# A delta-rule attention and a multiplicative FFN on one core: a new list of the early steps, and the last product's two token blocks summed and stored one by one

## The chip, the cores and the metric

The kernel runs on one core of one Trainium2 chip. The metric is device time in microseconds of one execution, and the time of a kernel is the median of its runs. One of the executions of the kernel before was recorded by the profiler; all durations below come from that one.

## What is computed

Two blocks follow each other. The first is a delta-rule recurrence over 768 time steps, for 4 batches of 8 heads with 48 features; the second multiplies the result, as 3072 tokens of 384 features, with four weights.

```
k_n = k / (norm(k) + 1e-6)
for t in range(768):
    y[t] = q[t] @ state
    v_old = k_n[t] @ state
    state += beta[t] * outer(k_n[t], v[t] - v_old)
x = y as (3072 tokens, 384)
a, b = x @ w1, x @ w2                  # 384 x 1024 each
out = ((a * b) @ w3) @ w_out           # 1024 x 1024, 1024 x 384
```

All data are float32.

## The kernel before

**Tiling.** The sequence is cut into 12 chunks of 64 time steps. Two chunks make a unit, so there are six units, of 512 tokens each. Within a chunk the recurrence is solved in matrix form: scores K K^T and Q K^T, the inverse of a triangular matrix, and a chain that carries the state from chunk to chunk. In the FFN, `w3 @ w_out` is folded once into one weight `w34` of 1024 x 384, so that a unit needs the two products with w1 and w2 (eight column slabs of 128), their elementwise product, and one product with `w34`. That last product is done in a scheme with seven half-size products in place of eight (`slab_sums`, `weight_sums`, `o`), whose results are combined by additions in `result`.

**One list sets the order on every engine.** The kernel is a set of Python generators, one for each piece of work, and the string `ORDER` (line 39) names which of them does its next step. `in_text_order` (line 159) then ties every engine's instructions to the order of the text. So an engine that waits for one step holds up all later steps of its own queue. SyncE (SP), which issues nearly all DMAs, is such a queue too. The names in the list:

- `P0` to `P7`: a 128-row piece of w_out; `P8` to `P23`: half of a 128-row block of w3; `P24` to `P29`: pieces of w1, `P30` to `P35`: pieces of w2 (`piece`, line 695). Each piece has four steps: its DMA into a buffer `raw`; two activations on ScalarE (ACT, lines 707 and 708); two operations on VectorE (DVE, lines 710 and 711); an addition on GpSimd (POOL, line 715). There are five `raw` buffers in turn, so that the load of a piece waits until the POOL step of the piece five places before it is done.
- `t`: transposes of w3 on TensorE (PE), `f0` to `f7`: the folds into `w34` (line 756), each in two halves; the first half needs P0 to P3, the second P4 to P7.
- `k`, `q`, `v`, `p`: loads of a chunk; `K`, `Q`, `d`: the transposed keys and queries, by PE for the first two chunks, by DVE later; `g` and `N`: squared norms and their inverse roots.
- `s`: scores; they leave `U` (DVE, line 379) and the masked `PT` (ACT copy and POOL multiplication for the first two chunks). `u`: `U` to DRAM in blocks; `V0` to `V5`: the triangular inverse of a unit, 31 pairs of DVE operations (lines 440 and 445), after a load of `Ub` and followed by a store of `Vd`; `e`: the rest of the inverse, which begins with eight DMAs from `Vd`.
- `n`: values times norms (POOL); `c`: the chain; `y`: a chunk's outputs on PE, eight ACT copies into `xT`, and six small DMAs within `xT` (line 684).
- `b0` to `b7`: a slab of unit 0 for chunk 0 alone (N = 256 columns); `a00` to `a07`: the same for chunk 1; `a10` and so on: a slab of a later unit, both chunks (line 772).
- `T`: the weight sums, `S`: the slab sums (both POOL), `o`: the seven products of a unit (line 851), `x`: their sums and stores (`result`, line 896).

**The end.** For the last unit `o` puts the products named E and F into two-bank PSUM buffers of their own. `store` (line 880) takes the next of two SBUF buffers `osb`, lets `make` fill its 384 columns (two token blocks of 192), and issues two DMAs, one for each token block. Of the last unit's four stores, three are sums on DVE, one after the other: U3 + C, U3 - D, and M1 + F, where F is the product that PE does last.

Of the kernel before, what the change touches and what calls it, by code (L numbers as in the profile page):

```python
# [45 lines left out]
P16 V0 f0 f1 P14 t11 V0 V0 f0 f1 v1 P15 P15 v0 P15 t6 t11 V0 V0 V0 V0 P16 f5 V0 P20 g1 P22 s1
P21 t8 P23 P22 t6 d2 f5 f5 P20 d2 P20 V0 P21 P15 n0 t7 P24 V0 f3 V0 t9 t8 V0 t7 t9 s2 P20 V0 n0
V0 f4 p3 n1 P22 P23 V0 V0 V0 P23 g1 d3 V0 V0 P22 g1 f3 t14 P23 f4 f3 t12 t14 P30 f4 p3 g1 V0
t15 n1 t12 P26 s1 g1 g1 f6 f7 e0 d3 N1 e0 t15 e0 P21 e1 N1 f7 e0 P21 p4 s2 d3 P24 s2 P24 e0 s2
e1 s2 e0 s2 d3 e1 P30 e1 c0 c0 f7 s3 V1 u2 P26 y0 t13 P24 P26 s3 P31 s3 P26 N1 P30 P30 y0 s3  # L50
P25 c0 P31 P25 s3 u3 s3 c0 t13 e1 c1 P31 e1 c1 P32 V1 c1 P25 V1 P28 c1 P31 V1 V1 V1 V1 V1 V1 V1
f6 V1 V1 P32 V1 V1 P32 y0 f6 V1 V1 V1 P25 P28 P28 V1 V1 v2 y1 b2 b2 b0 P32 y1 b3 b3 P27 P29 b3
b0 b0 V1 b0 b1 y1 c1 k4 a00 b1 P28 b3 P29 n2 P29 P27 P27 V1 a01 P33 a00 a00 a03 P27 V1 V1 V1 V1
a00 a02 V1 P29 V1 V1 V1 V1 a01 a03 V1 V1 b5 g2 P33 P34 a02 b5 b7 k5 a07 b2 V1 V1 P35 a06 b7 V1
b2 p4 b6 P34 g2 a06 a07 V1 n2 a04 V1 b4 b6 P33 P35 a05 g2 P34 b4 b1 c1 g2 V1 P34 a04 e2 P35 a01
P33 P35 a05 g2 a01 e3 T d4 e2 a03 c2 e2 b1 c2 e2 g2 d4 d4 g2 a04 T p5 e2 e2 d4 a05 g2 a03 a04
c2 s4 c2 g2 b5 g2 p5 a05 N2 b4 s4 s4 c2 a06 b5 c2 b4 a07 y2 d5 y2 s4 d5 T b7 s4 a02 s4 a06 b6
S0 d5 e3 v3 d5 a02 T a07 b6 S0 e3 e3 n3 V2 n3 s5 k6 g3 b7 s5 s5 S0 S0 g3 o0 c3 u4 c3 s5 N2 e3
e3 s5 S0 g3 s5 u5 x0 S0 S0 V2 o0 S0 c3 S0 c3 S0 S0 o0 x0 y3 x0 V2 V2 S0 V2 V2 V2 g3 y3 N2 o0 S0
v4 o0 c3 V2 V2 x0 V2 V2 V2 S0 V2 y3 o0 V2 S0 x0 x0 p6 V2 x0 x0 a10 V2 x0 S0 o0 V2 x0 V2 V2 a10  # L60
a16 a16 a15 a12 p6 V2 V2 a10 a11 a12 V2 k7 V2 V2 v5 g3 V2 V2 V2 a15 V2 a11 V2 a14 a17 V2 a10 x0
V2 V2 V2 d6 a12 a17 d6 g3 V2 g3 g3 e4 a14 d6 e4 a17 e4 a13 c3 c4 n5 a17 e4 a12 n4 V3 n4 g3 p7
d6 e4 g3 c4 e4 n5 a14 s6 N3 a13 s6 c4 a11 s6 a14 c4 c4 p7 y4 c4 e5 d7 a15 e5 y4 k8 e5 c5 c5 g4
d7 g4 a13 a16 e5 d7 d7 a15 a13 v6 a16 a11 s7 e5 S1 g4 g4 s7 o1 p8 s7 S1 e5 x1 s7 s7 S1 s7 c5 o1
s6 S1 u7 c5 o1 s6 s6 u6 S1 S1 V3 S1 y5 c5 c5 V3 V3 V3 V3 V3 o1 S1 x1 k9 S1 y5 S1 y5 o1 S1 S1 x1
x1 V3 S1 S1 V3 c6 V3 S1 S1 V3 d8 o1 x1 x1 v7 a20 n6 x1 V3 a20 o1 x1 a23 V3 V3 x1 V3 x1 n7 a27
a24 d8 a26 V3 V3 V3 V3 x1 g4 V3 a23 V3 a25 V3 a27 a27 V3 a24 V3 V3 a26 a20 V3 g4 V3 p8 V3 V3 V3
V3 p9 V3 V3 a25 d8 n6 d8 g4 a20 a22 a22 a24 V3 c6 a27 a25 a24 a21 a21 e6 e6 e6 g4 e7 N3 e6 a25
N3 g4 s8 g4 N4 s8 e6 a22 s8 a26 e6 c6 c6 N4 s8 a26 s8 y6 a22 V4 p9 N4 S2 d9 e7 s8 a21 e7 y6 u8
d9 a21 e7 c6 a23 d9 p10 e7 d9 S2 c6 S2 s9 n7 a23 s9 e7 o2 s9 c7 s9 S2 s9 k10 S2 c7 x2 o2 c7 S2  # L70
S2 o2 u9 s9 V4 c7 V4 S2 y7 V4 V4 x2 V4 g5 g5 V4 p10 d10 y7 S2 x2 S2 o2 y7 V4 o2 x2 c7 V4 V4 S2
S2 V4 o2 a35 x2 x2 k11 x2 S2 V4 x2 S2 a35 v8 V4 S2 V4 V4 S2 V4 x2 n8 o2 a37 x2 V4 v9 V4 V4 V4
x2 a34 n8 V4 V4 a36 a30 V4 V4 V4 V4 V4 a37 V4 a34 a33 V4 g5 a33 a30 a32 a36 V4 V4 V4 V4 a34 a33
V4 V5 a32 e8 n9 c7 e8 a30 c8 a33 e8 e9 e8 g5 a35 a34 c8 a30 e8 g5 d10 a32 e9 g5 a32 g5 a36 e8
e9 S3 c8 a36 a35 a31 d10 d10 e9 a31 n9 c8 g5 c8 c8 g5 g5 e9 a31 s10 N5 e9 p11 s10 s10 a31 c9
a37 a37 p11 c9 y8 N5 v11 d11 S3 d11 d11 o3 v10 d11 s10 y8 s10 S3 u10 S3 s11 N5 s11 o3 s10 c9
s11 c9 s11 S3 x3 S3 s11 o3 S3 S3 y9 o3 s11 x3 S3 o3 u11 V5 S3 S3 V5 y9 V5 x3 n11 S3 x3 V5 V5 V5
S3 y9 S3 S3 V5 c9 V5 o3 x3 V5 x3 x3 V5 V5 x3 S3 a47 o3 x3 V5 V5 a47 x3 V5 V5 a47 n10 V5 a46 a40
a40 V5 a47 V5 a43 V5 a46 x3 a42 a45 V5 a42 V5 a41 a45 a43 V5 V5 V5 V5 V5 V5 a44 V5 a44 V5 a45
a41 V5 V5 V5 V5 c9 a42 e10 a40 e10 n11 a42 e10 a44 e10 c10 a45 n10 e11 e10 e11 c10 a43 e10 c10  # L80
c10 a40 e11 a41 a46 e11 c10 a44 S4 a43 e11 a41 S4 c10 o4 e11 a46 c11 x4 S4 S4 y10 o4 c11 c11 S4
y10 S4 S4 S4 S4 S4 c11 o4 y11 o4 x4 S4 S4 S4 o4 y11 x4 x4 o4 S4 x4 x4 S4 y11 S4 x4 x4 a50 x4 o4
a50 x4 a55 a56 a55 a52 a55 a50 a52 a56 a54 a57 a54 a55 a54 a50 a54 a51 a52 a57 a51 a53 x4 a52
a53 a51 a56 a56 a53 a51 a53 a57 o5 S5 a57 S5 S5 o5 S5 S5 S5 x5 S5 S5 S5 o5 o5 x5 S5 S5 S5 o5 S5
S5 S5 o5 x5 S5 x5 o5 x5 x5 x5 x5 x5 x5 x5 x5
"""


# [1 line left out]
def kernel(  # L90
# [799 lines left out]

    last = NCH // 2 - 1

    def bank_of(u, n):
        return banks[u, n].rearrange("p b d -> p (b d)")

    def result(u):
        def plus(x, n, op=ALU.add):
            return lambda o_: dve.tensor_tensor(  # L898
                out=o_, in0=ws_[x], in1=bank_of(u, n), op=op
            )  # L900
# [134 lines left out]
```

## Time and profile before

| | us |
|---|---|
| median of 3 runs (591.1 to 597.29) | 592.53 |
| the profiled execution | 597.89 |
| its span, from first to last instruction | 596.2 |
| PE busy in the span | 545.3 |
| DVE busy in the span | 363.5 |
| ACT busy in the span | 158.8 |
| POOL busy in the span | 176.3 |
| matmuls with w1 and w2 (line 779), busy | 129.6 and 131.4 |
| matmuls of the seven products (line 873), busy | 65.0 and 49.6 |

The profiled execution lies 1.69 us over its span, and 5.36 us over the median of the three runs. The matmuls of line 779 are single instructions of 538 ns, pipelined, so that their busy times overlap a little. The page also gives the busy share of every engine in 40 slices of about 15 us; there DVE, POOL and the DMA engines are at their busiest in the first ten slices and PE from the tenth slice on.

### The profile page before, as it was taken

The numbers are of one execution on the slowest core, as the hardware profiler recorded it, in microseconds if no ns is written. First come the engines' busy times: TensorE is split into PE (matmuls) and PEld (weight loads), VectorE is DVE, ScalarE is ACT, GpSimd is POOL, SyncE is SP. The second block draws the span as 40 slices with busy tenths as digits, with TensorE's granted clock in tenths as the row PEclk, the third lists the DMA queues.
The fourth block names the chain that finished last, engine by engine and source line by source line (L and its number), as shares of the span: only waits on it lengthen the run. The fifth ranks groups of instructions, "written<-read, shape, count | busy, mean of one in ns | idle before, by whom it ended". The sixth has DMA issues, their size and how long they took to land.

```text
span 596.2 us, 19061 instructions
## 1 busy us (share of the span) xinstructions
PE 545.3 (91%) x8188; PEld 381.0 (64%) x8188; DVE 363.5 (61%) x827; ACT 158.8 (27%) x333; POOL 176.3 (30%) x223
## 2 busy tenths in 40 slices
PE   2477999578999999999999989999999999999996
...
DVE  3887997568877579665697555875746924110012
...
PEclk9998999878999899999999999999999999999999
DMA  9989986776856255553463345614333040010001
GB/s 247 186 175 266 216 155 132 129 156 120 166 81 101 70 103 93 99 92 50 110 112 73 53 70 98 130 47 72 57 65 90 13 89 4 16 46 8 1 0 53
DMA packets 219507, 57.31 MB, mean 96 GB/s; under 512 B 206656, under 2 KB 212800, under 8 KB 219424
## 3 DMA queue, kind: packets, MB, share of 16 engines
...
q10 hardware_dynamic: 4192, 0.79, 0.9%
...
## 4 chain that ended last, share of the span: by engine, by line
PE 78%; DMA 10%; SPq 5%; DVE 3%; issue 2%; ACT 1%; POOL 1%; ACTq 0%; DVEq 0%; POOLq 0%
PE ps_f L779 41%; PE ps_f L873 19%; PE ps_w L551 5%; DMA raw<-in_moe_w_dram 4%; PE ps_w L652 4%; PE ps_f L759 3%; PE ps_w L498 3%; SPq L230 2%; PE ps_w L367 2%; PE ps_w L373 2%; DMA ktok<-in_k_dram 1%; DMA Ub<-Ud 1%; DMA Ud<-U 1%; SPq L699 1%; DMA X<-in_q_dram 1%
## 5 line engine op out<-in xcount | busy, mean ns | idle before, releaser
L779 PE MATMUL ps_f<-xT,w1s 128*128 128x512 f32 (+1 forms) x336 | 129.6, 538 | 2.6 <-DMA xT<-xT 2.6
L779 PE MATMUL ps_f<-xT,w2s 128*128 128x512 f32 (+1 forms) x336 | 131.4, 537 | 0.0
L846 POOL TENSOR_TENSOR ab<-ab 128x256 f32<-128x256 f32 x96 | 67.1, 727 | 193.6 <-DVE ab L795 167.8
L779 PEld LDWEIGHTS ps_f<-xT,w1s 128*128 128x128 f32 x336 | 64.3, 193 | 58.1 <-issue 53.7
L779 PEld LDWEIGHTS ps_f<-xT,w2s 128*128 128x128 f32 x336 | 62.2, 190 | 53.7 <-issue 50.2
L791 ACT COPY ab<-ps_f 128x512 f32<-128x512 f32 (+1 forms) x56 | 28.3, 526 | 172.3 <-PE ps_f L779 168.1
L873 PE MATMUL ps_f<-w,ab 128*128 128x192 f32 x368 | 65.0, 330 | 0.0
L795 DVE TENSOR_TENSOR ab<-ab,ps_f 128x512 f32<-128x512 f32 (+1 forms) x56 | 32.7, 603 | 48.8 <-PE ps_f L779 48.6
L873 PEld LDWEIGHTS ps_f<-w,ab 128*128 128x128 f32 x368 | 59.7, 190 | 3.9 <-issue 2.9
L440 DVE TENSOR_TENSOR tb<-Vb,Ub 128x31 f32<-128x31 f32 (+15 forms) x124 | 45.8, 370 | 14.3 <-DMA Ub<-Ud 10.9
L873 PE MATMUL ps_f<-room,ab 128*128 128x192 f32 x272 | 49.6, 337 | 0.8 <-DVE room L898 0.8
L759 PE MATMUL ps_f<-w2s,w3T 128*128 128x384 f32 x128 | 46.3, 515 | 3.4 <-POOL w2s L715 3.3
L445 DVE TENSOR_TENSOR Vb<-Vb,tb 128x31 f32<-128x31 f32 (+15 forms) x124 | 46.4, 374 | 4.3
L873 PEld LDWEIGHTS ps_f<-room,ab 128*128 128x128 f32 x272 | 45.8, 195 | 1.6 <-issue 1.1
L673 ACT COPY xT<-ps_w 48x256 f32<-48x256 f32 x96 | 30.4, 365 | 52.5 <-PE ps_w L652 52.0
L759 PEld LDWEIGHTS ps_f<-w2s,w3T 128*128 128x128 f32 x128 | 24.7, 200 | 20.3 <-POOL w2s L715 4.2
L270 POOL TENSOR_TENSOR sq<-ktok 128x384 f32<-128x384 f32 x24 | 20.6, 863 | 57.6 <-DMA ktok<-in_k_dram 27.5
L367 PE MATMUL ps_w<-KQ 48*64 48x128 f32 x384 | 30.4, 298 | 1.1 <-ACT KQ L347 1.1
L373 PE MATMUL ps_w<-KQ 48*64 48x64 f32 x768 | 30.7, 236 | 0.0
L715 POOL TENSOR_TENSOR w<-w,raw 128x512 uint32<-128x512 uint32 x16 | 20.8, 1307 | 32.2 <-DVE w L711 13.5
L537 POOL TENSOR_TENSOR vtok<-vtok,n 128x384 f32<-128x384 f32 x24 | 20.1, 849 | 33.7 <-DMA vtok<-in_v_dram 33.7
L373 PEld LDWEIGHTS ps_w<-KQ 48*64 48x64 f32 x768 | 27.8, 149 | 0.1
...
## 6 DMA issues: line engine op xcount, KB each, us to landing
...
```

Source lines behind the costliest of these rows:

```text
L367: pe.matmul(ps[half(z), 0, n : n + 128], lhsT=x[:, 0, :], rhs=x.rearrange("p j t -> p (j t)"), start=True, stop=True,)
L373: pe.matmul(ps[half(z ^ j), 1, n + C * j : n + C * j + C], lhsT=x[:, 0, :], rhs=x[:, j, :], start=True, stop=True,)
L440: dve.tensor_tensor(out=tv, in0=V[:, 0 : s + 1, s : s + 1].to_broadcast([P, s + 1, n]), in1=U[:, s, s + 1 : BS].unsqueeze(1).to_broadcast( ...
L445: dve.tensor_tensor(out=o, in0=o, in1=tv, op=ALU.subtract)
L551: pe.matmul(out(ps, r, h, z), lhsT=lhs(r, h, z), rhs=rhs(r, h, z), start=True, stop=True,)
L673: act.copy(out=xT[f, p:NP:2, b : b + NR, cc, :].rearrange("p a r t -> p r a t"), in_=pyv[f, z, b : b + NR],)
L759: pe.matmul(ps[:, 0:DM], lhsT=w3Ts[jc, kc // 4][:, kc % 4 * P : kc % 4 * P + P], rhs=wo[:, kc], start=(kc == 0), stop=(kc == KF - 1),)
L779: pe.matmul(ps[:].rearrange("p b c t -> p b (c t)"), lhsT=w[:, m, js], rhs=x[:, m, :, c0:c1].rearrange("p b c t -> p b (c t)"), start=(m = ...
L791: act.copy(out=t, in_=ps)
L795: dve.tensor_tensor(out=t, in0=t, in1=ps, op=ALU.mult)
L846: pool.tensor_tensor(out=o_, in0=x_, in1=y_, op=op)
L873: pe.matmul(ps[:, b, :], lhsT=abs_[u, HF * f + i][:, t0 : t0 + P], rhs=ws_[w][:, i], start=first and b == i == 0, stop=i == HF - 1 and b = ...
```

## The change

The list in `ORDER` is another one up to a place in the middle of unit 1's products and the first of its outputs; after it the names are the same ones in the same order, but for one more `x5` at the end. No name appears more or less often in the early part, so every instruction of it is still there; only the order on the engines is another.

On the engines this comes to the following. **SP:** nearly the same order of transfers. What differs: a piece of w_out changes places with pieces of w3 among the first loads, and two pieces of w_out stand after the permuted loads `p2`, not before them; one piece of w1 stands ahead of `u2`; `k4` and `k5` stand after the pieces P33 to P35; later the DMAs of `e4` and `e5` stand together, ahead of loads that were between them. **The pieces** of one kind are taken in another sequence: before P6 P10 P8 P2 P11 P13 P12 P18 P9 P7 P1 P3 P0 P5 P4, after P0 P18 P13 P11 P10 P3 P12 P8 P9 P2 P5 P1 P4 P6 P7. **PE:** the first halves of f1, f0 and f2 stand together ahead of the first second half (before: f1, f2, then the second half of f2); after y1 the six half-slab products are b3 b1 b0 b1 b2 b3 (before b2 b0 b3 b3 b0 b1). **ACT:** P15 stands after the copies of f1 and t11 (before after f2, f0 and f1); P30 stands ahead of e0's first copies; e1's last copies stand directly after P25 and P31 (before t13 lay between). **DVE:** seven pieces stand between the first and the last pair of V0 (before eight). **POOL:** V0's two memsets stand ahead of the first piece (before after the first two products of g0); the pieces P25 and P30 stand ahead of s1's second mask multiplication.

The core of the list, its first lines:

```diff
-k0 P6 beta P10 P6 beta P6 P8 P6 P2 P11 K0 P10 P13 k1 P10 K0 P2 beta P11 q0 P10 P12 g0 P2 P8 P11
-g0 g0 P13 K1 V0 g0 P2 P12 K0 P8 P11 K0 K0 K1 K1 P8 g0 P12 P13 g0 Q0 g0 g0 g0 Q0 Q0 P13 P18 g0
-Q0 P9 Q0 K1 P12 s0 k2 P18 N0 q1 s0 K1 P7 P1 g1 s0 s0 P9 g1 Q1 Q1 Q1 Q1 P18 Q1 s0 s0 s0 P7 P18
+V0 P0 k0 beta P18 P13 P0 P18 P0 P0 P18 P18 g0 P11 beta P13 K0 K0 P11 P10 q0 P10 P3 k1 P11 P13
+K0 beta P12 g0 P3 K0 g0 K0 g0 P13 K1 g0 P8 P12 g0 K1 K1 P11 P9 Q0 Q0 g0 Q0 P10 P12 g0 Q0 Q0 g0
+k2 K1 s0 g0 P9 P10 P8 N0 K1 q1 P2 s0 N0 P3 Q1 s0 P12 p2 g1 Q1 P2 N0 s0 s0 Q1 P9 Q1 P8 Q1 g1 s0
...
```

The second part of the change is in `o`, `store` and `result`. F's two token blocks go into two PSUM banks, each with its own start and stop; the sum M1 + F is made and stored in two parts of 192 columns, into the buffer of U2, which no one reads any more then, and not into an `osb`.

```diff
-            if first and n in "EF":
-                banks[u, n] = two_banks()[:, 0, 0 : HB * HD].rearrange(
-                    "p (b d) -> p b d", b=HB
-                )
-            elif first:
-                banks[u, n] = bank([P, HB, HD])[:]
+            if first:
+                ps = [bank([P, HB, HD])[:]] * HB if n not in "EF" else [
+                    two_banks()[:, 0, 0 : HB * HD].rearrange("p (b d) -> p b d", b=HB)
+                ] * HB
+                if n == "F":
+                    ps[0] = bank([P, HB, HD])[:]
+                banks[u, n] = ps
...
-                        start=first and b == i == 0,
-                        stop=i == HF - 1 and b == HB - 1, skip_group_check=not first,
+                        start=first and i == 0 and (b == 0 or n == "F"),
+                        stop=i == HF - 1 and (b == HB - 1 or n == "F"),
+                        skip_group_check=not first,
...
-    def store(u, z, d, make):
-        osb = in_turn(ffn, [P, DM], "o", 2, "osb")
-        make(osb[:])
-        yield
-        for b in range(HB):
-            t0 = (HB * z + b) * S + u * 2 * C
-            sync.dma_start(
-                out=out[t0 : t0 + P, d_half(d)], in_=osb[:, HD * b : HD * b + HD]
-            )
-        yield
+    def store(u, z, d, make, osb=None, parts=1):
+        if osb is None:
+            osb = in_turn(ffn, [P, DM], "o", 2, "osb")[:]
+        n = DM // parts
+        for i in range(0, DM, n):
+            make(osb[:, i : i + n], slice(i, i + n))
+            yield
+            for b in range(i // HD, (i + n) // HD):
+                t0 = (HB * z + b) * S + u * 2 * C
+                sync.dma_start(
+                    out=out[t0 : t0 + P, d_half(d)], in_=osb[:, HD * b : HD * b + HD]
+                )
+            yield
...
-        yield from store(u, 0, 1, plus("M1", "F") if u == last else plus("U2", "C"))
+        if u == last:
+            yield from store(u, 0, 1, plus("M1", "F"), ws_["U2"], HB)
+        else:
+            yield from store(u, 0, 1, plus("U2", "C"))
```

More of the change, by code (lines that the diff above doesn't have):

```diff
@@ L39 @@
 ORDER = """
-k0 P6 beta P10 P6 beta P6 P8 P6 P2 P11 K0 P10 P13 k1 P10 K0 P2 beta P11 q0 P10 P12 g0 P2 P8 P11
-g0 g0 P13 K1 V0 g0 P2 P12 K0 P8 P11 K0 K0 K1 K1 P8 g0 P12 P13 g0 Q0 g0 g0 g0 Q0 Q0 P13 P18 g0
-Q0 P9 Q0 K1 P12 s0 k2 P18 N0 q1 s0 K1 P7 P1 g1 s0 s0 P9 g1 Q1 Q1 Q1 Q1 P18 Q1 s0 s0 s0 P7 P18
-g1 P3 P9 t2 P7 s1 s1 s1 s1 s1 s1 P7 P1 t2 P3 t5 P1 p2 d2 N0 t5 N0 P0 P0 P3 P0 u0 P9 d2 u1 P1 P3
-P5 t1 P4 g1 P0 t0 V0 V0 t0 P19 t1 t10 t3 P5 t4 V0 P14 P16 f1 P5 V0 V0 V0 V0 V0 P4 P4 V0 t10 t4
-f2 V0 P19 V0 t3 P14 P5 P14 P19 P17 P17 k3 s0 p2 P4 P16 V0 P17 V0 V0 V0 V0 f2 f2 f0 P17 V0 P19
@@ L46 @@
[L46 to L85, printed above, removed]
+V0 P0 k0 beta P18 P13 P0 P18 P0 P0 P18 P18 g0 P11 beta P13 K0 K0 P11 P10 q0 P10 P3 k1 P11 P13
+K0 beta P12 g0 P3 K0 g0 K0 g0 P13 K1 g0 P8 P12 g0 K1 K1 P11 P9 Q0 Q0 g0 Q0 P10 P12 g0 Q0 Q0 g0
@@ new lines @@
+k2 K1 s0 g0 P9 P10 P8 N0 K1 q1 P2 s0 N0 P3 Q1 s0 P12 p2 g1 Q1 P2 N0 s0 s0 Q1 P9 Q1 P8 Q1 g1 s0
+P3 s0 t2 t2 t3 s1 P5 P8 P2 g1 s1 P2 P1 s1 s1 t3 P9 P5 s1 P4 s1 P5 u0 P5 s1 d2 P1 P4 t1 u1 t0 P6
+t4 P7 t1 t10 P1 t0 t5 V0 t4 P14 g1 V0 P1 t10 P6 f1 t5 V0 d2 P4 P6 V0 V0 V0 P7 V0 P7 V0 P16 P14
+V0 P4 V0 P19 P19 P19 P6 f0 P16 P17 P17 V0 V0 P16 V0 V0 P17 P7 f2 k3 P14 p2 V0 V0 v1 P19 P15 f1
+f0 g1 f1 t11 V0 d2 t11 P15 f2 f5 V0 P14 P15 f0 P16 v0 P17 V0 V0 V0 V0 g1 P20 f5 V0 f2 f5 t6 t9
+P15 t6 P20 t7 V0 n1 P22 P20 V0 t7 d2 s0 V0 V0 f3 P23 P20 P22 t8 P21 V0 n0 P24 n0 f3 V0 V0 n1 t8
@@ new lines @@
+V0 V0 t9 V0 V0 s2 p3 f4 f3 P23 P22 P26 g1 V0 g1 V0 f4 g1 P21 P22 P23 t14 d3 f4 P23 g1 t12 p3 V0
+N1 P30 t12 t14 t15 e0 t15 d3 f7 d3 f6 e0 P30 P21 e0 e0 P24 f7 s2 s2 e1 e0 s2 P24 e0 e1 V1 p4 s2
+e1 P26 s2 e1 P25 d3 c0 P21 P30 u2 s3 c0 s3 P26 N1 P31 P24 y0 s3 s3 y0 c0 s3 s3 P25 t13 N1 e1 u3
+P31 c0 P26 P31 P32 c1 V1 c1 e1 P25 V1 P27 c1 V1 c1 V1 V1 t13 V1 V1 V1 V1 V1 V1 y0 V1 P25 f7 f6
+f6 P30 P32 P32 v2 V1 P27 s1 P31 V1 V1 y1 b3 b1 V1 b0 P32 P28 y1 b1 V1 b1 b3 P29 P27 b2 b3 y1 V1
+P27 b1 b0 P29 P29 c1 a01 b2 a03 P28 V1 a01 a00 b3 P28 P29 a02 a02 a03 P35 P28 V1 a05 b7 a00 V1
@@ new lines @@
+V1 V1 V1 a06 P33 V1 b5 a05 b7 b0 V1 P34 V1 b5 V1 a06 V1 V1 V1 P34 k4 V1 P35 V1 g2 a00 V1 k5 a00
+b0 V1 V1 g2 a04 P34 n2 p4 n2 a07 c1 a04 b2 b4 P33 b6 b2 P35 V1 g2 g2 P34 g2 e2 a07 g2 P33 e2
+P35 c2 c2 e3 d4 a03 d4 a03 a01 P33 g2 b4 d4 g2 e2 b6 e2 a07 e2 b4 d4 T a01 T b4 e2 a07 c2 s4 p5
+g2 c2 T g2 N2 V2 b6 p5 b6 s4 b5 s4 c2 a06 c2 a06 a04 v3 y2 d5 b5 d5 k6 s4 e3 d5 s4 y2 a02 a05
+d5 s4 b7 a04 n3 S0 a02 a05 S0 s5 S0 u4 e3 s5 n3 s5 e3 b7 T o0 c3 c3 s5 g3 s5 S0 N2 N2 x0 e3 g3
+e3 o0 s5 c3 c3 u5 o0 x0 V2 S0 x0 y3 V2 y3 S0 V2 S0 V2 S0 S0 V2 V2 V2 S0 g3 o0 S0 o0 S0 x0 V2 c3
@@ new lines @@
+o0 v4 y3 V2 V2 V2 x0 p6 V2 x0 V2 S0 a10 a10 S0 g3 S0 x0 V2 x0 S0 o0 x0 x0 p6 a14 V2 k7 a17 a17
+a14 V2 V2 V2 a15 a16 V2 a16 a15 V2 g3 V2 V2 V2 V2 V2 v5 V2 x0 a13 V2 V2 V2 a17 a12 V2 a13 g3 V2
+V2 g3 a17 c3 a14 a13 d6 d6 a11 V2 e4 n4 a12 e4 e4 c4 d6 V3 e4 a14 a10 n4 g3 d6 c4 e5 a11 e4 s6
+g3 a13 e4 a12 p7 a10 c4 g3 N3 s6 c4 s6 a11 y4 n5 y4 c4 e5 a12 c4 a11 a15 c5 n5 e5 p7 a16 d7 d7
+d7 d7 o1 c5 v6 a16 k8 g4 g4 e5 g4 p8 a15 g4 s7 s7 S1 e5 s7 S1 e5 x1 s7 s7 S1 s7 c5 o1 s6 S1 u7
+c5 o1 s6 s6 u6 S1 S1 V3 S1 y5 c5 c5 V3 V3 V3 V3 V3 o1 S1 x1 k9 S1 y5 S1 y5 o1 S1 S1 x1 x1 V3 S1
@@ new lines @@
+S1 V3 c6 V3 S1 S1 V3 d8 o1 x1 x1 v7 a20 n6 x1 V3 a20 o1 x1 a23 V3 V3 x1 V3 x1 n7 a27 a24 d8 a26
+V3 V3 V3 V3 x1 g4 V3 a23 V3 a25 V3 a27 a27 V3 a24 V3 V3 a26 a20 V3 g4 V3 p8 V3 V3 V3 V3 p9 V3
+V3 a25 d8 n6 d8 g4 a20 a22 a22 a24 V3 c6 a27 a25 a24 a21 a21 e6 e6 e6 g4 e7 N3 e6 a25 N3 g4 s8
+g4 N4 s8 e6 a22 s8 a26 e6 c6 c6 N4 s8 a26 s8 y6 a22 V4 p9 N4 S2 d9 e7 s8 a21 e7 y6 u8 d9 a21 e7
+c6 a23 d9 p10 e7 d9 S2 c6 S2 s9 n7 a23 s9 e7 o2 s9 c7 s9 S2 s9 k10 S2 c7 x2 o2 c7 S2 S2 o2 u9
+s9 V4 c7 V4 S2 y7 V4 V4 x2 V4 g5 g5 V4 p10 d10 y7 S2 x2 S2 o2 y7 V4 o2 x2 c7 V4 V4 S2 S2 V4 o2
@@ new lines @@
+a35 x2 x2 k11 x2 S2 V4 x2 S2 a35 v8 V4 S2 V4 V4 S2 V4 x2 n8 o2 a37 x2 V4 v9 V4 V4 V4 x2 a34 n8
+V4 V4 a36 a30 V4 V4 V4 V4 V4 a37 V4 a34 a33 V4 g5 a33 a30 a32 a36 V4 V4 V4 V4 a34 a33 V4 V5 a32
+e8 n9 c7 e8 a30 c8 a33 e8 e9 e8 g5 a35 a34 c8 a30 e8 g5 d10 a32 e9 g5 a32 g5 a36 e8 e9 S3 c8
+a36 a35 a31 d10 d10 e9 a31 n9 c8 g5 c8 c8 g5 g5 e9 a31 s10 N5 e9 p11 s10 s10 a31 c9 a37 a37 p11
+c9 y8 N5 v11 d11 S3 d11 d11 o3 v10 d11 s10 y8 s10 S3 u10 S3 s11 N5 s11 o3 s10 c9 s11 c9 s11 S3
+x3 S3 s11 o3 S3 S3 y9 o3 s11 x3 S3 o3 u11 V5 S3 S3 V5 y9 V5 x3 n11 S3 x3 V5 V5 V5 S3 y9 S3 S3
@@ new lines @@
+V5 c9 V5 o3 x3 V5 x3 x3 V5 V5 x3 S3 a47 o3 x3 V5 V5 a47 x3 V5 V5 a47 n10 V5 a46 a40 a40 V5 a47
+V5 a43 V5 a46 x3 a42 a45 V5 a42 V5 a41 a45 a43 V5 V5 V5 V5 V5 V5 a44 V5 a44 V5 a45 a41 V5 V5 V5
+V5 c9 a42 e10 a40 e10 n11 a42 e10 a44 e10 c10 a45 n10 e11 e10 e11 c10 a43 e10 c10 c10 a40 e11
+a41 a46 e11 c10 a44 S4 a43 e11 a41 S4 c10 o4 e11 a46 c11 x4 S4 S4 y10 o4 c11 c11 S4 y10 S4 S4
+S4 S4 S4 c11 o4 y11 o4 x4 S4 S4 S4 o4 y11 x4 x4 o4 S4 x4 x4 S4 y11 S4 x4 x4 a50 x4 o4 a50 x4
+a55 a56 a55 a52 a55 a50 a52 a56 a54 a57 a54 a55 a54 a50 a54 a51 a52 a57 a51 a53 x4 a52 a53 a51
@@ L86 @@
+a56 a56 a53 a51 a53 a57 o5 S5 a57 S5 S5 o5 S5 S5 S5 x5 S5 S5 S5 o5 o5 x5 S5 S5 S5 o5 S5 S5 S5
+o5 x5 S5 x5 o5 x5 x5 x5 x5 x5 x5 x5 x5 x5 x5
 """
@@ L873, in o, with make @@
                     pe.matmul(
-                        ps[:, b, :], lhsT=abs_[u, HF * f + i][:, t0 : t0 + P], rhs=ws_[w][:, i],
-                        start=first and b == i == 0,
-                        stop=i == HF - 1 and b == HB - 1, skip_group_check=not first,
+                        ps[b][:, b, :], lhsT=abs_[u, HF * f + i][:, t0 : t0 + P],
+                        rhs=ws_[w][:, i], start=first and i == 0 and (b == 0 or n == "F"),
+                        stop=i == HF - 1 and (b == HB - 1 or n == "F"),
+                        skip_group_check=not first,
                     )
             yield
-    def store(u, z, d, make):
-        osb = in_turn(ffn, [P, DM], "o", 2, "osb")
-        make(osb[:])
-        yield
-        for b in range(HB):
-            t0 = (HB * z + b) * S + u * 2 * C
-            sync.dma_start(
-                out=out[t0 : t0 + P, d_half(d)], in_=osb[:, HD * b : HD * b + HD]
-            )
-        yield
+    def store(u, z, d, make, osb=None, parts=1):
[11 more added lines that the diff above has]
+            yield
     last = NCH // 2 - 1
     def bank_of(u, n):
-        return banks[u, n].rearrange("p b d -> p (b d)")
+        return banks[u, n][-1].rearrange("p b d -> p (b d)")
     def result(u):
         def plus(x, n, op=ALU.add):
-            return lambda o_: dve.tensor_tensor(
-                out=o_, in0=ws_[x], in1=bank_of(u, n), op=op
-            )
+            def make(o_, c=slice(0, DM)):
+                y = banks[u, n][c.start // HD].rearrange("p b d -> p (b d)")[:, c]
+                dve.tensor_tensor(out=o_, in0=ws_[x][:, c], in1=y, op=op)
+            return make
         act.copy(out=ws_["M1"], in_=bank_of(u, "A"))
         yield
-        yield from store(u, 0, 0, lambda o_: act.copy(out=o_, in_=bank_of(u, "A")))
+        yield from store(u, 0, 0, lambda o_, c: act.copy(out=o_, in_=bank_of(u, "A")))
         plus("M1", "B")(ws_["U2"])
```

## The prediction

> **What bounds the kernel now.** I read the page's slices first, then the sums by stage, the chain of waits, SP's own waits, and the last 11 us instruction by instruction.
>
> Slices of 14.9 us, tenths of busy time:
>
> ```profile
> PE   2477999578999999999999989999999999999996
> DVE  3887997568877579665697555875746924110012
> PEclk9998999878999899999999999999999999999999
> DMA  9989986776856255553463345614333040010001
> ```
>
> From the tenth slice on PE is full. Only the first ten slices and the last leave it room. The sums by stage put numbers on the worst two stretches (time, PE busy, weight loads, DVE, ACT, POOL, granted clock, DMA share, GB/s):
>
> ```profile
> 105.00:120.00 15.00, 6.92 (x332) 5.74 (x320) 8.60 (x17) 5.21 (x14) 2.65 (x3) 0.87 0.75 128
> 120.00:135.00 15.00, 11.69 (x217) 9.10 (x218) 10.54 (x28) 8.31 (x19) 2.49 (x3) 0.79 0.76 161
> ```
>
> PE idles there with work still on the list. The chain of waits says for what (start, us, who; this view leaves its small pieces out):
>
> ```profile
> 56.98 12.29 PE ps_f L759 x32
> 69.77 0.58 ACT w L707
> 70.83 0.70 DVE w L711
> 71.76 1.29 POOL w L715
> 73.07 5.73 DMA raw<-in_moe_w_dram
> 78.82 0.60 SPq L230
> ...
> 88.53 3.26 DMA Vd<-Vb
> ...
> 130.94 6.35 DMA raw<-in_moe_w_dram
> 137.35 0.64 SPq L684
> 138.05 0.63 SPq L684
> 138.73 1.70 SPq L684
> 140.54 0.58 SPq L684
> 141.48 2.12 DMA xT<-xT
> 143.74 23.31 PE ps_f L779 x100
> ```
>
> The reader sees a queue, not an engine, as the bound: folds on PE, then the steps of piece P15, whose POOL step frees a `raw` buffer; then SP loads P24, goes through the permuted loads, stores Vd (DVE had ended V0 at 85.2, ACT copied until 86.3; SP came at 88.5), and at last issues y1's six `xT` transfers, whose data ACT had ready at 135.9. At 143.7 PE gets them and is full from then on: its gaps from 144 to the end sum to 5.5 us, the largest 1.9, 1.3 and 0.8. So the early list is worth what it moves the 143.7, and whatever holes it makes or fills after it. SP's own waits up to 143 us (total, times, longest) show where it loses time to the `raw` buffers:
>
> ```profile
> SPq L699 <- POOL w L715: 8.7, 4, 4.4
> SPq L699 <- POOL w2s L715: 3.0, 3, 1.6
> ```
>
> In the last slice PE ends its last product (588.45 + 2.76 = 591.2), and DVE sums it late:
>
> ```profile
> 589.59 1.01 DVE L898 TENSOR_TENSOR osb<-room,ps_f 128x384 f32<-128x384 f32 x2
> 592.39 0.55 DVE L898 TENSOR_TENSOR osb<-room,ps_w 128x384 f32<-128x384 f32 x1 [1.79 <-DMA out_dram<-osb]
> ```
>
> It waits 1.79 us for an `osb` that a store still reads.
>
> [...]
>
> **The change part by part.**
>
> *SP.* The order of transfers is almost the old one and their number is the same, so bytes and issue times are equal. What can move is how long SP waits for `raw` buffers. First place: before, SP stood from 15.6 to 20.8 because P18's buffer waited for P8's POOL step (19.53 + 1.28); k2 and q1 stood behind it, and so chunk 1's scores, `u1` and V0. After, the two loads there are P8 and P9, which wait for P13's and P11's POOL steps. From the old rows: ACT can take the third load at about 11.5 and the fourth at 13; DVE does both after K0's copy at 13.1, four operations of 0.43 to 0.69, until about 15.9; POOL does P13 at 16.0 to 17.3, one square (0.83), P11 until 19.4. V0's memsets (0.95 + 0.32), now ahead of P0, shift P0's POOL step from 7.4 to 8.6, which only the load of P3 feels. So SP is 1.3 to 1.7 us earlier at k2. On its way PE does one more transpose group (1.0) between the scores; V0's DVE work starts about 1.0 earlier (51.1 for 52.1). *Second place:* P24 waits for P15's POOL step. After, P15 stands on ACT behind f1 and t11, not behind f2, f0 and f1. With the three first halves together (3 x 2.75 from 47.5) PE reaches f1's second half at 55.8, when P7 is through POOL (before it waited 2.87 for P4); f1 ends at 58.5, f0 at 61.2, t11 at 62.6. Then it is P15's load that counts: issued at 62.4, at most 6.3 to landing as before (63.4 to 69.7). ACT by 69.3 at worst, DVE 1.1, POOL 1.3: SP goes on at 70.9 to 71.8, and not 73.1. That is -1.3 to -2.2. V0 itself: 22.5 us of pairs, seven pieces of 1.06 for eight, one reduction of 0.5 more: it ends near 83.5, and ACT near 84.6. SP's work from P24 to Vd is the same 15.4 us, so Vd goes at 86.3 to 87.2: SP stays the bound.
>
> *From Vd to xT.* e0 and c0 follow at once with the same steps. P30 on ACT ahead of e0's copies costs 0 if its load lands 6 us after its issue at 87, and up to 2 if it takes 8. Piece P25 ahead of u2 on SP costs `u2` 1.8, but u2 is wanted only by V1, with u3. e1's last copies wait for the second of two loads as before (4.0 us of PE wait at c1), but this load is now issued 1.9 plus the shift sooner, so y1 can be ready at about 132 to 133. SP gets to y1's transfers after the same number of issues: at about 135.3 for 137.4. So the 143.7 becomes 141.7: I take **-2.0**, with -4.5 and +1.5 as its ends.
>
> *After xT.* Ahead of it PE has done the same work in both (six half slabs, c1), so the shift counts in full. Behind it every engine's order differs up to unit 1, while PE has as much to do; 1.3 + 0.5 us of old gaps can go or grow. I take 0, ends -1 and +3. Costed at nothing: `k4` and `k5` behind three pieces are some 5 us later, but what needs them last is N2 (DVE at 175.0 before, over 20 us behind the loads); `e5`'s eight DMAs ahead of `p7` delay it by some 5 us under a PE that is full; should that cover fail, each us is one of PE.
>
> *The end.* The 1.79 us wait goes, since U2's buffer is free once DVE, the same engine, has read it. E, C, U3 + C and U3 - D stay as they are until 590.6; then block 0's sum, 590.65 to 591.0, and block 1's after PE's 591.2, until 591.6. But SP is next: before, it issued the four DMAs ahead at 590.17, 590.54, 591.07 and 591.50, each 0.33 to 0.43 long. Block 0's bank is A's, which ACT had read by 581.3, so PE waits for nothing. The last two stores come at about 591.98 and 592.4, ending 592.8 for 593.8 (592.97 + 0.81). The landing behind it is the same 2.4 (596.2 - 593.8). So **-1.0**, not the -1.8 of the wait; ends -0.6 and -1.5. That the sum is in two parts is worth almost nothing, SP being behind.
>
> *The sum:* -2.0 + 0 - 1.0 = -3.0. The profiled execution took 597.89 and would take 594.9. The median of the runs is 592.53, 5.4 less; the steps hold there alike: 589.5.
>
> **The rivals.** *Likeliest, 0.52:* small gains as above, 586.5 to 592.5. *The buffers' waits fall away, 0.28:* the 11.7 us that SP loses to POOL are what holds the front; if the new sequence takes away half of them and none comes back (K0's copies no longer stand behind P12's load on ACT, so Q0 and the scores can go 2 us sooner), the front gains 5.5 to 6, with the end 7: 585.5. For it: SP is the bound at both places of the chain. Against: the loads themselves are full-rate early, and a wait on a buffer becomes a wait for a landing. *A new hole, 0.15:* after xT, PE's fifth product is a05 (before b5 at the sixth), whose weights need P28. P28's DVE step stands behind sixteen pairs of V1 and the products b1 and b3, by my count at 141.7, POOL until 143.0, while PE comes to a05 at 141.7 + 6 = 147.7. Up to 4.7 us late costs nothing. Ub took 5.9 us before; if it takes that once more and V1 starts 10 us late, PE stands 5.3, and b7, a06 and b5 behind it. With a front that gained nothing, some 5 us at the clock of 0.8 that such a gap brought before (+1), and S and T late on POOL (+1), it is 5.3 + 1 + 1 - 1.0 = +6.3: 598.8. It decides from the point where P28's addition ends after 147.7. *The list changes nothing that counts, 0.05:* only the end remains, 591.5.
>
> **How the numbers follow.** A run of this kernel scatters over 6 us, so about 1% (586.6 to 598.5) is what can be told from no change. The likeliest case lies within it by nearly all its weight, the second mostly below (0.22 of its 0.28, with 0.08 from the first), the third above with 0.08, and scatter alone with 0.02. Faster 0.31, within 0.59, slower 0.10. The range takes in the second case's centre and some of the scatter and ends short of the third's centre: 584 to 597.
>
> **What would show it.** Right: V0's first pair near 51, Vd's store near 86.7, the big block of line 779 from about 141.7, no DVE wait at the last sum, SP's last issue 1.6 us after PE's end. Wrong: SP's waits for POOL of 11.7 us unchanged; V0 not earlier; a PE gap of over 2 us between 142 and 200; or a first block of line 779 before 139, which is the second rival's.

## The result

| | before | after |
|---|---|---|
| median of 20 runs each, us | 595.95 | 595.2 |
| lowest to highest | 591.1 to 599.0 | 590.6 to 598.65 |
| the profiled execution | 597.89 | 593.18 |
| its span | 596.2 | 591.5 |

The ratio after to before is 0.9983, with a 95% interval from 0.9962 to 1.0005: -1.0 us, between -2.3 and +0.3. The forecast was -3.0. The two profiled executions differ by 4.7 us, and that is not the change: each is one draw from a scatter of 8 us.

**The profile after.** The slices that were shown of the kernel before:

```profile
PE   2569898778999999999999989999999999999997
DVE  3897898569986579574796545865746924110012
PEclk9988999679999999999999999999999999999999
DMA  9989986668856455563553345614432040010001
```

PE is at nine tenths only from the eleventh slice on, as before (the tenth slice shows 8 in both), and the DMA engines are as full in the first six (tenths 9 9 8 9 9 8 in both). The weak stretches in the sums by stage (time, PE, weight loads, DVE, ACT, POOL, granted clock, DMA share, GB/s):

```profile
105.00:120.00 15.00, 9.89 (x355) 8.86 (x345) 6.58 (x12) 4.28 (x11) 1.28 (x1) 0.64 0.71 127
120.00:135.00 15.00, 12.05 (x218) 9.23 (x219) 11.16 (x29) 9.86 (x23) 5.51 (x5) 0.79 0.71 166
```

PE is busy 21.9 us of these 30 for 18.6 before, but in the first stretch at a clock of 0.64 for 0.87 and with 355 matmuls for 332. The same matmuls took longer there (those of line 373 269 ns each for 220), so most of the rise is slower work, not more of it. The longest transfers in the chain of waits of after (start, us, who):

```profile
62.54 5.74 DMA raw<-in_moe_w_dram
...
88.78 4.90 DMA raw<-in_moe_w_dram
...
121.11 6.09 DMA Ub<-Ud
...
134.47 5.19 DMA raw<-in_moe_w_dram
```

From 93 us on the chain is mostly SP's issues and such landings. Between 68 and 88 us it runs over V0's pairs on DVE, by a link that does not hold: the wait for POOL that it names ends at 89.1, and the load it should have released had started at 88.78. SP was still the later one at Vd:

```profile
84.00 1.07 ACT L449 COPY Vb<-ps_w 128x512 f32<-128x512 f32 x2 [2.68 <-DVE ps_w L445]
```

V0's copies had ended at 85.07, and SP came to its store at 88.24. So the bound is of the same kind: SP and the landings it waits for. The last additions of after, on DVE:

```profile
585.77 1.01 DVE L905 TENSOR_TENSOR osb<-room,ps_f 128x384 f32<-128x384 f32 x2
586.70 0.35 DVE L905 TENSOR_TENSOR room<-room,ps_f 128x192 f32<-128x192 f32 x1
587.43 0.35 DVE L905 TENSOR_TENSOR room<-room,ps_w 128x192 f32<-128x192 f32 x1 [0.39 <-PE ps_w L874]
```

and the last stores, on SP:

```profile
586.34 1.77 SPq L891 DMA_DIRECT2D out_dram<-osb  x4
588.21 0.86 SPq L891 DMA_DIRECT2D out_dram<-room  x2
```

The wait of 1.79 us for a buffer is gone; DVE waits only for PE now, and the stores follow each other on SP without a pause. The early landmarks and the end were then read in eight profiles, four with the old list (before twice, and two experiments below) and four with the new one.

### The profile page after: what moved, and what is told of

Read it like the earlier page. It is cut to its first block, busy times and chain, and to the rows that moved or that the text cites. A ratio compares the mean times of both kernels' runs of the same rounds, so it can differ in the third digit from the quotient of the medians.

```text
span 591.5 us, 19063 instructions
## 1 busy us (share of the span) xinstructions
PE 542.2 (92%) x8188; PEld 379.8 (64%) x8188; DVE 363.0 (61%) x828; ACT 159.3 (27%) x333; POOL 176.3 (30%) x223
## 4 chain that ended last, share of the span: by engine, by line
PE 70%; SPq 10%; DMA 9%; DVE 5%; issue 2%; ACT 1%; POOL 1%; DVEq 0%; POOLq 0%; ACTq 0%
PE ps_f L779 38%; PE ps_f L874 19%; DMA raw<-in_moe_w_dram 5%; PE ps_w L551 5%; PE ps_w L652 4%; SPq L230 3%; SPq L699 2%; PE ps_w L498 2%; DMA ktok<-in_k_dram 2%; DVE tb L440 1%; SPq L202 1%; DVE ps_w L445 1%; PE ps_w L367 1%; DMA Ub<-Ud 1%; PE ps_w L373 1%
## 5 line engine op out<-in xcount | busy, mean ns | idle before, releaser
L779 PE MATMUL ps_f<-xT,w1s 128*128 128x512 f32 (+1 forms) x336 | 128.0, 532 | 2.0 <-DMA xT<-xT 2.0
L874 PE MATMUL ps_f<-w,ab 128*128 128x192 f32 x376 | 66.3, 330 | 0.0
L874 PEld LDWEIGHTS ps_f<-w,ab 128*128 128x128 f32 x376 | 61.2, 190 | 4.2 <-issue 3.3
L874 PE MATMUL ps_f<-room,ab 128*128 128x192 f32 x272 | 48.0, 330 | 0.8 <-DVE room L905 0.8
L874 PEld LDWEIGHTS ps_f<-room,ab 128*128 128x128 f32 x272 | 44.1, 190 | 1.6 <-issue 1.1
L270 POOL TENSOR_TENSOR sq<-ktok 128x384 f32<-128x384 f32 x24 | 20.7, 866 | 70.0 <-DMA ktok<-in_k_dram 39.5
```

The lines of the kernel that those rows point to most:

```text
L779: pe.matmul(ps[:].rearrange("p b c t -> p b (c t)"), lhsT=w[:, m, js], rhs=x[:, m, :, c0:c1].rearrange("p b c t -> p b (c t)"), start=(m = ...
L874: pe.matmul(ps[b][:, b, :], lhsT=abs_[u, HF * f + i][:, t0 : t0 + P], rhs=ws_[w][:, i], start=first and i == 0 and (b == 0 or n == "F"), s ...
```

## The experiments

Theory A is the prediction's: the list is worth -2.0, the end -1.0. B: the end is all of it. C: the list costs time. Ratios are to the kernel before on the same chip.

### One half of the change alone

*list_only* has the new list (with 13 `x5`) and the old `o`, `store` and `result`. *tail_only_2* has the new ones with the old list, to which it adds the two `x5` that the stores in two parts need. (The changed list has 14 `x5` for 12: two more, not one.) Its last line against before:

```diff
-S5 S5 o5 x5 S5 x5 o5 x5 x5 x5 x5 x5 x5 x5 x5
+S5 S5 o5 x5 S5 x5 o5 x5 x5 x5 x5 x5 x5 x5 x5 x5 x5
```

*tail_only* adds one `x5` only and so leaves out the last token block's store.

> The new list with the old last sum and stores. Theory A expects -2.0 us, ratio 0.9966. Theory B expects 0, ratio 1.000: the 1.4 us that SP has gained at P24 are lost again until Vd, and P25 ahead of u2 costs P31 what is left. Theory C expects +1, ratio 1.0015. From PE's end to the span's end 5.0 us in all.

> The old list with the new last sum and stores. Theory A (the prediction: list -2, end -1.0) expects -1.0 us, ratio 0.998. Theory B (the end is all of the change, the list is worth 0) expects -0.9, ratio 0.9985, and from PE's end to the span's end 4.1 us where before it is 5.0. Theory C (the list costs time and the end is worth the whole 1.8 us wait) expects -1.8, ratio 0.997.

> Old list, new end, with both x5 steps so that every token block is stored. Theory 'the end is all of it': ratio 0.9985 against before (-0.9 us), the time from TensorE's last matmul to the span's end 4.1 us. Theory of the prediction (list -2.0, end -1.0): the same -1.0 here, and about 2 us slower than the changed kernel. Theory 'the list costs': 0.997 (-1.8 us).

Measured: list_only 0.9995 (0.9973 to 1.0016), so -0.3 us, from -1.6 to +0.95. tail_only_2 0.9987 (0.9964 to 1.0010), -0.8 us; tail_only 0.9975 (0.9946 to 1.0004), with a store less. The intervals of a ratio are wider than the end's effect, but the time from PE's last matmul to the span's end hardly scatters:

| | us from PE's end to the span's end |
|---|---|
| before, before_again, list_only | 4.95, 4.94, 4.96 |
| after, tail_only_2 | 4.07, 4.08 |
| tail_only, with one store less | 3.57 |
| u2_one_part (below) | 4.07 |
| osb_two_parts (below) | 4.75 |

The end is worth -0.9 us, and the list -0.3 (from its own run) or -0.2 (0.9983 less 0.9987, known only to about 1.9 us). A's -2.0 for the list lies outside list_only's interval. B fits, though a gain of up to 1.6 us from the list is not excluded; C, which needs -1.8 from the end, falls.

### Which part of the end

*u2_one_part* leaves F in one bank and sums it at once into U2's buffer:

```diff
-                if n == "F":
-                    ps[0] = bank([P, HB, HD])[:]
...
-            yield from store(u, 0, 1, plus("M1", "F"), ws_["U2"], HB)
+            yield from store(u, 0, 1, plus("M1", "F"), ws_["U2"])
```

*osb_two_parts* keeps the two banks and the two parts, but sums into an `osb`:

```diff
-            yield from store(u, 0, 1, plus("M1", "F"), ws_["U2"], HB)
+            yield from store(u, 0, 1, plus("M1", "F"), None, HB)
```

> The changed kernel, but F in one bank, summed once and stored into U2's buffer with one pair of stores behind it: the wait for an osb is gone, the parts are not. If SP's queue is the bound at the end (A and B), from PE's end to the span's end it takes at most 0.3 us more than the changed kernel's 4.1. If the two parts are what counts, 5.0 as before.

> The changed kernel with F in two banks and two parts, but into an osb again: the wait is back, the parts stay. If the wait is what counts, 5.0 us from PE's end to the span's end, less some 0.2 for the shorter second sum; if the parts count, 4.1.

DVE's last additions in osb_two_parts:

```profile
588.00 0.35 DVE L905 TENSOR_TENSOR osb<-room,ps_f 128x192 f32<-128x192 f32 x1 [1.79 <-DMA out_dram<-osb]
588.27 0.35 DVE L905 TENSOR_TENSOR osb<-room,ps_w 128x192 f32<-128x192 f32 x1
```

The old wait of 1.79 us is back, and with it 0.7 of the 0.9 us. With one part in U2 nothing is lost (4.07 for 4.07). So the buffer is the gain; the two parts are worth 0.2 us without it and nothing beside it, since SP is still issuing the four stores ahead when the first part is ready.

### How far the landmarks move by themselves

> The kernel before, profiled once more, nothing changed: it tells how far the landmarks of the old list move by themselves from one execution to the next. Theory 'the list is worth nothing': V0's first pair at 52 again, Vd and e0 within 1 us of 88 and 95, the same as in the four profiles of the new list. Theory 'the list is worth 2 us': Vd and e0 at 88.5 and 95.4 or later.

The profile met neither theory: V0's first pair came at 50.8, Vd at 86.8 and e0 at 94.1, all of them early. One more execution could not decide. With four and four profiles (old: before, before_again, tail_only, tail_only_2; new: after, list_only, u2_one_part, osb_two_parts), start times in us:

| | old list, mean (range) | new list, mean (range) | shift |
|---|---|---|---|
| SP at k2 | 21.4 (21.0 to 21.8) | 20.7 (20.2 to 21.4) | -0.8 |
| V0's first pair | 51.65 (50.8 to 52.1) | 50.8 (50.7 to 51.0) | -0.85 |
| P24's load | 72.3 (71.1 to 73.1) | 71.6 (70.7 to 72.0) | -0.7 |
| `kperm`, behind P24 | 74.1 (72.9 to 74.9) | 73.4 (72.5 to 73.8) | -0.7 |
| `kperm`'s fourth transfer | 77.5 (76.0 to 78.6) | 77.8 (77.0 to 78.4) | +0.3 |
| the raw load behind `kperm` | 81.8 (80.5 to 83.4) | 81.7 (81.0 to 82.0) | -0.1 |
| Vd's store | 88.2 (86.8 to 89.8) | 87.9 (87.1 to 88.2) | -0.3 |
| e0 on DVE | 95.3 (94.1 to 97.0) | 95.1 (94.2 to 95.7) | -0.2 |
| y1's `xT` on SP | 135.6 (134.0 to 137.4) | 134.5 (133.6 to 135.9) | -1.1 |
| PE full, at that `xT` | 141.3 (139.9 to 143.7) | 139.9 (139.1 to 141.6) | -1.4 |

The standard error of a shift grows from 0.3 at V0's start over 0.7 at Vd to 0.9 and 1.0 in the last two rows. Only V0's earlier start is clear of the scatter; at `xT` and at PE the means are earlier by about one standard error, which neither shows a gain nor excludes one of 2 us. Before's profile had been the latest of its four at `xT` (137.4), and before_again the earliest (134.0), with the same instructions. In the means the shift is gone in the `kperm` transfers. SP's queue there in after:

```profile
65.01 8.50 SPq L699 DMA_DIRECT2D raw<-in_moe_w_dram  x8
73.55 8.25 SPq L230 DMA_DIRECT2D kperm<-in_k_dram  x8
81.90 1.82 SPq L699 DMA_DIRECT2D raw<-in_moe_w_dram  x4
83.82 4.33 SPq L230 DMA_DIRECT2D qperm<-in_q_dram  x8
88.24 0.43 SPq L453 DMA_DIRECT2D Vd<-Vb  x1
```

and in before:

```profile
65.31 9.50 SPq L699 DMA_DIRECT2D raw<-in_moe_w_dram  x8
74.85 7.07 SPq L230 DMA_DIRECT2D kperm<-in_k_dram  x8
82.02 1.82 SPq L699 DMA_DIRECT2D raw<-in_moe_w_dram  x4
83.89 4.54 SPq L230 DMA_DIRECT2D qperm<-in_q_dram  x8
88.53 0.43 SPq L453 DMA_DIRECT2D Vd<-Vb  x1
```

The raw loads came 1.3 us sooner to their end, and `kperm` gave 1.2 of it back. SP's waits from 65 to 83 us name what it stood for (total, times, longest), in after

```profile
SPq L230 <- DMA raw<-in_moe_w_dram: 3.7, 3, 2.6
```

and in before

```profile
SPq L230 <- DMA raw<-in_moe_w_dram: 2.1, 2, 1.4
```

SP's permuted loads wait for raw loads to land: 2.1 to 3.2 us in the four old profiles, 3.2 to 3.7 in the new. No data ties the two. The trace gives with every issue the semaphore (a counter that others can wait on) that tells of its landing: this program has eight of them, which SP's and ACT's transfers take in turn; in before and after, from the 27th transfer in the text on, the same one comes every eight places. In these two traces no transfer started before the one that had its semaphore last had landed (548 of 548 pairs with a landing on record in each), so each one stands for the landing of the transfer eight places ahead of it. For `kperm`'s fourth that is the load just ahead of P24. In before it landed 8.53 us after its issue, so at 77.72:

```profile
69.19 0.42 SPq L699 DMA_DIRECT2D raw<-in_moe_w_dram  x1
77.73 0.31 SPq L230 DMA_DIRECT2D kperm<-in_k_dram  x1
```

In after it took 9.34 us, until 78.37:

```profile
69.03 0.38 SPq L699 DMA_DIRECT2D raw<-in_moe_w_dram  x1
78.38 0.31 SPq L230 DMA_DIRECT2D kperm<-in_k_dram  x1
```

SP had issued this load before it stood for P24's buffer, so going on sooner at P24 does not by itself make it land sooner. At the first place, 12 to 25 us, the same happened. Before:

```profile
SPq L699 <- POOL w L715: 4.4, 1, 4.4
```

After:

```profile
SPq L699 <- DMA X<-in_q_dram: 4.2, 1, 4.2
SPq L699 <- POOL w L715: 0.5, 1, 0.5
```

A wait of 4.4 to 5.4 us for POOL in the old profiles has become one of 4.1 to 4.3 us for `X` in the new: ACT issues that load of `X`, and in after it has the semaphore (103) that SP's raw load takes next.

### Would a shift at Vd count?

Three kernels move only SP's transfers around V0's store. In the three diffs the removed line is a stretch of the changed kernel's list. *vd_first* puts the store (the last `V0` there) ahead of `qperm` (the second step of `p3`):

```diff
-P23 t14 d3 f4 P23 g1 t12 p3 V0 N1 P30 t12 t14 t15 e0 t15
+P23 V0 t14 d3 f4 P23 g1 t12 p3 N1 P30 t12 t14 t15 e0 t15
```

*vd_e0_first* also puts e0's first eight loads ahead of P30:

```diff
-P23 t14 d3 f4 P23 g1 t12 p3 V0 N1 P30 t12 t14 t15 e0 t15
+P23 V0 t14 d3 f4 P23 g1 t12 p3 N1 e0 P30 t12 t14 t15 t15
```

*vd_late* puts the store behind P30:

```diff
-P23 t14 d3 f4 P23 g1 t12 p3 V0 N1 P30 t12 t14 t15 e0 t15
+P23 t14 d3 f4 P23 g1 t12 p3 N1 P30 t12 t14 t15 V0 e0 t15
```

> The changed kernel, V0's store to DRAM put on SyncE's queue ahead of the eight transfers of qperm (4.3 us of issues) and not behind them; nothing moves on another engine. The store then goes out when ScalarE's copies are done, at 84.8 to 85.8 us for 88.2; the raw load behind it still waits for GpSimd (90.9), so e0's loads start at 91.5 as before or a little earlier. Theory 'SyncE's queue up to e0's loads sets e0': e0 0 to 1 us sooner, since its loads stand behind that raw load; ratio 0.998.

> As the run before, and e0's first eight loads ahead of P30's raw load. Loads at about 90 for 91.5 to 95.9; e0's first eight T loads 1.5 us sooner, P30 4 us later. Theory of the prediction (a shift at this place counts in full): V1, y1 and TensorE's start at xT 1.5 us sooner, ratio 0.9958. Theory 'the stretch after e0 takes a shift back, SyncE's transfers for raw and kperm being the pace': the start at xT within 1 us of the changed kernel's mean of 139.9, ratio 0.998, P30's delay perhaps making it 0.999 to 1.002.

> The changed kernel with V0's store behind P30's raw load: it goes out at about 91 us for 88.2, and e0's loads, which wait for its landing (3.3 us), at about 94.2 for 91.5. Theory of the prediction (a shift here counts in full): the start at xT 2.7 us later, ratio 1.003 (+4.5 thousandths on the changed kernel's 0.9983). Theory 'the stretch after e0 takes it back': start at xT and time as in the changed kernel, ratio 0.998 to 0.999.

Measured: vd_late 1.0028 (1.0010 to 1.0045), so 4.5 thousandths or 2.7 us above the changed kernel's 0.9983, give or take 1.7. SP's queue in vd_late:

```profile
86.67 2.13 SPq L699 DMA_DIRECT2D raw<-in_moe_w_dram  x4
88.89 0.37 SPq L453 DMA_DIRECT2D Vd<-Vb  x1
92.62 1.92 SPq L462 DMA_DIRECT2D TT<-Vd  x4
```

In this one execution V0 was early (its last pair at 82.1), so the store's own time looks harmless; what counts is that from the start of V0's last pair to e0 it took 13.8 us, for 11.7 in the mean of the four unaltered profiles of the new list. So the delay here, of e0 and of all that stands behind it on SP, was about 2.1 us, and the time rose by about as much: **a delay at e0 counts, as far as this can be measured in full.** That is the prediction's rule, and one kernel supports it; the list delivered no shift there that stands out of the scatter. The single profile, though, doesn't show the delay at `xT` (136.1, within the spread of the eight); the verdict rests on the ratio.

In the other direction less came. vd_first: 0.9990 (0.9969 to 1.0011), which takes in the 0.998 expected; in its profile the store went out at 86.8, later than expected, and from V0's last pair to e0 it took 12.6 us, so no gain. vd_e0_first:

```profile
84.34 0.35 SPq L453 DMA_DIRECT2D Vd<-Vb  x1
84.79 4.78 SPq L230 DMA_DIRECT2D qperm<-in_q_dram  x8
89.61 2.08 SPq L462 DMA_DIRECT2D TT<-Vd  x4
```

The loads went out at 89.6, as expected, and V0's last pair to e0 took 11.2 us, 0.5 less than the mean of 11.7. The ratio is 0.9975 (0.9962 to 0.9988): under before by 0.25%, but not told apart from the changed kernel (0.9983). The 0.9958 of the theory that a shift counts in full lies outside, but it was for a shift of 1.5 us, and 0.5 came. It has the lowest ratio of the complete kernels and is the only one with an interval wholly below 1, the best of nine, so that some luck may be in it.

### Filling SP's wait

*kperm_early* puts the eight transfers of `kperm` ahead of P24's load, into SP's wait for its buffer:

```diff
-P20 P22 t8 P21 V0 n0 P24 n0 f3 V0 V0 n1 t8 V0 V0 t9 V0 V0 s2 p3 f4
+P20 P22 t8 P21 V0 n0 p3 P24 n0 f3 V0 V0 n1 t8 V0 V0 t9 V0 V0 s2 f4
```

> The changed kernel with the eight transfers of kperm (4 us of issues) put ahead of P24's raw load on SyncE and not behind it; nothing else moves. SyncE stands 2.3 us there for P24's buffer, and in the kperm transfers another 3 to 4 us for the landing of raw loads. Theory 'these waits of SyncE are what ate the list's earlier start': the transfers fill the wait, V0's store goes out at 85.5 to 86.5 us for 88.2, e0 and TensorE's start at xT come 1.5 to 2.5 us sooner, ratio against before 0.995. Theory 'P24 is what counts': its load starts 2 to 3 us later, and the products behind it; ratio 1.000 to 1.003. Theory 'nothing up to e0 counts': 0.998.

Its queue on SP:

```profile
64.55 4.12 SPq L699 DMA_DIRECT2D raw<-in_moe_w_dram  x4
68.72 10.66 SPq L230 DMA_DIRECT2D kperm<-in_k_dram  x8
79.47 3.68 SPq L699 DMA_DIRECT2D raw<-in_moe_w_dram  x8
83.25 4.67 SPq L230 DMA_DIRECT2D qperm<-in_q_dram  x8
88.02 0.43 SPq L453 DMA_DIRECT2D Vd<-Vb  x1
```

The wait for P24's buffer is gone (P24's load follows at once), and Vd goes out at 88.0 all the same: `kperm` took 10.66 us for 8.25, single issues up to 4.3 us. Ratio 0.9978 (0.9954 to 1.0001), as the changed kernel. The first theory as written, that these waits ate the shift and can be filled, fails: the trace names no wait there, the issues themselves took longer. From 60 to 75 us the DMA engines are busy 0.96 to 1.00 in before, after and this kernel, at 220 to 235 GB/s. That the drain of these bytes paces SP fits this stretch in all three, but from 76 to 80 us the engines of kperm_early were at six tenths or less while SP was still at `kperm`, and a kernel with fewer bytes at this place wasn't tried, so it isn't shown.

### Issuing from another queue

*xt_on_act* lets ScalarE issue y0's and y1's `xT` transfers (line 684) behind its own copies:

```diff
-                    sync.dma_start(
+                    (act if u == 0 else sync).dma_start(
```

*vd_xt_on_act* has this and lets it issue V0's store too (line 453):

```diff
-        sync.dma_start(out=Vds[j][:], in_=Vb[:])
+        (act if j == 0 else sync).dma_start(out=Vds[j][:], in_=Vb[:])
```

In the list these steps move up to stand directly behind ACT's copies; in vd_xt_on_act e0's first loads also stand ahead of P30.

> The changed kernel with the first unit's transfers of xT for y0 and y1 issued by ScalarE behind its own copies and not by SyncE. Theory 'SyncE's issue queue sets when xT starts': the issue moves from 134-136 us to 131-133, TensorE is full 2 to 3 us sooner, and the time falls by 2 to 3 us against the changed kernel (ratio against before about 0.995). Theory 'the landing or the later weights set it': the issue moves but TensorE's start doesn't, ratio 0.9985 as the changed kernel.

> As the run before, and V0's store to DRAM is issued by ScalarE directly behind the copies, too. Theory 'the earlier start of V0 is lost in SyncE's queue ahead of the Vd store': Vd goes out at about 85 us and not 88, e0 starts 2 to 3 us sooner, and another 1 to 3 us come off the time (about 0.992 against before). Theory 'e0 waits for something else, or what follows absorbs it': Vd moves, and e0 or TensorE's start at xT doesn't; ratio as in the run before.

All four theories missed: 1.0036 (1.0015 to 1.0058) and 1.0142 (1.0099 to 1.0186, with 6 runs, at a mean granted clock of 0.962 to 0.970 for 0.981 before, so that part of this may be slower work on PE). SP's waits in vd_xt_on_act from 84 to 136 us say why (its line 698 is the raw loads' line 699):

```profile
SPq L698 <- DMA xT<-xT: 7.5, 1, 7.5
SPq L698 <- DMA Vd<-Vb: 5.3, 1, 5.3
```

The transfers waited for, on ACT's queue, and the loads that waited, on SP's:

```profile
84.74 0.36 ACTq L452 DMA_DIRECT2D Vd<-Vb  x1
81.61 7.11 SPq L698 DMA_DIRECT2D raw<-in_moe_w_dram  x4
117.98 4.11 ACTq L683 DMA_DIRECT2D xT<-xT  x5
112.05 8.11 SPq L698 DMA_DIRECT2D raw<-in_moe_w_dram  x2
```

Vd did go out at 84.7, but two raw loads on SP, which have nothing to do with `xT` or Vd, stood until those transfers of ACT had landed: the waits' rows name them, 5.3 and 7.5 us. Half of the first wait and three quarters of the second passed before ACT had even issued the transfer: SP stood from 82.0 and from 112.4. e0 came at 96.3 and y1's `xT` at 142.4. These runs say nothing on what a faster SP would bring; they price the side effect.

## Why the prediction missed

**The end: right, for its own reason.** The forecast was -1.0; -0.9 was measured. SP being next in line, not the full 1.79 us, was right: SP's last issue ends at 588.69 + 0.38 = 589.07, 1.68 us after PE's end at 587.39, for 1.6 forecast. The 0.35 to 0.4 us in which the forecast lets DVE sum 192 columns were the author's estimate, since no row of before has that width; the rows of after show 0.35, where 384 columns took 0.55 in before. That the two parts are worth almost nothing is shown by u2_one_part. With the second bank DVE sums block 0 at 586.70, while PE is at work until 587.39; that one bank would not allow it was not shown. It is SP that makes no use of it.

**The front, first place: right in direction, about half in size at k2.** SP at k2 was to be 1.3 to 1.7 us sooner and is 0.8: the raw load ahead of k2 stood for `X` to land (at 19.29 in after), a wait that the sum did not have. V0's start, to be 1.0 sooner, is 0.85.

**The step that failed** is "SP's work from P24 to Vd is the same 15.4 us", and with it the counting of -2.0 in full. P24 itself was met (71.7 in after and 71.6 in the mean, for 70.9 to 71.8), but the 73.1 it was counted from was the latest of four: over four and four it is 0.7 sooner, not 1.3 to 2.2. And the 15.4 us were not only work: they held waits for landings. One of these shows in the prediction's own chain (73.07 + 5.73 = 78.80, and SP goes on at 78.82); the one ahead of it, at `kperm`'s fourth transfer, is for a load issued before P24 and does not move with P24. From P24 to Vd SP took 15.9 us in the mean of the four old profiles and 16.3 in the new, and a shift of -0.3 was left at Vd, for -1.3 to -2.2 forecast. The wait is in every profile of the eight; that it accounts for the whole difference is not shown, since shifts of 0.3 and 0.7 us lie within the scatter. The rival's own objection, that "a wait on a buffer becomes a wait for a landing", was the answer to the likeliest case as well, and was used only against the rival. SP's POOL waits "of 11.7 us unchanged" was named as a sign of error: after has 7.5 + 6.0 in the two groups that had 8.7 + 3.0, so they even rose.

**After Vd.** The rule that a shift there counts in full is supported by vd_late. "After xT 0" holds as far as this can be seen: from PE full at `xT` to PE's end it took 447.2 us in the mean of the four old profiles and 447.3 in the new, and no PE gap between 144 and 200 us is over 1 us in after, so the rival's hole at a05 did not open. P25 ahead of u2 moved `u2` from 107.6 to 109.9 and P31 from 109.8 to 113.7, and `xT` was still not late. The case given 0.05, that the list changes nothing that counts, is the one that came, as far as the intervals tell.

**A second fault is one of method.** Every size came from one execution whose `xT` stood at 137.4, where four of the same list average 135.6. So the landmark "the big block of line 779 from about 141.7" was met in after (141.59) by luck: the old list alone has it anywhere from 139.9 to 143.7.
